# A decay-attention and MoE kernel: the last tokens' scores of two heads with one low-part product, decay rows copied by GpSimd, and a new order for some casts

## The chip, the cores and the metric

The kernel runs on one core of one Trainium2 chip. The metric is device time in microseconds: the median of the runs, 1192.13 us before the change (three runs, 1192.12 to 1192.14).

## The reference

Attention with a learned decay over 8 batches of 8 heads, 576 tokens and head size 64, in fp32; its output, with the heads side by side, is the input of a token mixing of low rank (`U`, `V`) and of a two-layer ReLU network with 512 and 2048 columns.

```python
scores = scale * np.matmul(q, k.transpose(0, 1, 3, 2))
cum = np.cumsum(np.log(np.clip(f, 0.0001, 1.0)), axis=-1)
decay = cum[:, :, :, None] - cum[:, :, None, :]
scores = np.where(causal, -1000000000.0, scores + decay)
attn = softmax(scores)          # with 1e-09 added to the sum
x = attn @ v                    # heads put side by side
u = x + (x.T @ U @ V).T
out = u + np.maximum(u @ w_ch1, 0.0) @ w_ch2
```

## The kernel before

**Pairs and steps.** The 64 heads are worked off as 32 pairs `p`, four to a batch. One pair is one step `t` of ten slots `s` (`step`, L852); its two heads are `j` 0 and 1. In step `t` the scores of pair `p` are computed while the probabilities of pair `p-1` are transposed and multiplied with V, and the results of pair `p-2` are turned back. Between these, TensorE gets parts of the network of an earlier batch (`filler`: `A` and `B` matmuls) and, in seven "mixing" steps (6, 10, 14, 18, 22, 26 and 30), the token mixing of the batch just finished. When the last pair is done, at about 670 us, the rest of the network runs alone.

**Scores.** The 576 tokens of a head are four blocks of 128 (`MAIN` = 512) and a tail of 64 (`TAIL`). `score(p, j, i)` writes the scores of block `i` of head `j` into a PSUM bank: `S_00` to `S_03` in slots 0 to 3, `S_10` at the end of slot 6, `S_11` to `S_13` in slots 7 to 9. `score_tail(p, x)` computes the tails of both heads in one bank, head 0 in rows 0 to 63 and head 1 in rows 64 to 127; `x` is the half of the 576 keys, so each half has 288 columns (`St_0` in slot 4, `St_1` in slot 5). One matmul of head 0 and one of head 1 add up in the bank: the query columns of the other head are zero. Each bank then goes to VectorE (`top`, L388 for blocks, L414 for tails: scale, mask and maximum), and to ScalarE for the exponential (L396, and L424 for tails, which makes `Ptl`).

**Two ways to multiply.** Pairs 0 to 5 (`p < NF`) multiply plain fp32 tiles (L364; the trace shows two matmul records for one such matmul). From pair 6 on, scores are the sum of two fp32r products: `G[0]` and `G[1]` (`G_91` and `G_92` in lists of instructions) hold four planes of 576 columns for head 0 and head 1. Plane 0 is the high part of q, plane 1 the low part of q in the head's own 64 rows and decay values in 4 of the other rows, plane 2 the high and low part of k, plane 3 the high part of k in the own rows and decay values in 4 others. The high product is plane 0 by plane 2 (L367), the low product plane 1 by plane 3 (L368), so the low product also adds the decay.

**Who fills `G`.** `parts(p, j, engines)` casts q and k (L330) and subtracts for the low parts (L345, L346, 64x576 each on GpSimd). ScalarE makes the 128x576 casts, save for pairs 11, 15, 19, 23, 27 and 31, the pairs behind a mixing step, where GpSimd does. Head 0's planes of pair `p+1` are made from slot 6 of step `p` on, when the tail has last read `G[0]`; head 1's planes of pair `p` from slot 0 of step `p` on, for `S_10`. Two DMAs per pair (`place_decay`, L351) write the decay rows from a DRAM table `cumd`.

**What sets the order.** TensorE's instructions stand in the order of the code, and SyncE's (which issues the DMAs, `SP`) in step 0 and from step 7 on; those of ScalarE, VectorE and GpSimd are ordered when the kernel is built, by the times that a scheduler simulates, save where the code pins them. GpSimd also makes `VS` (L199), parts of the turned results `xh` and `xl` (L630, L631) and, behind mixing steps, casts of the network's input (`uh`, `ul`, L688 and L689). The weights are decoded on VectorE in steps 0 to 7 (L72 to L89).

## Time and profile before

| what | value |
|---|---|
| median of three runs | 1192.13 us |
| the profiled execution's own time | 1192.27 us |
| its span in the trace | 1190.5 us |
| PE (TensorE matmul), busy | 1173.5 us, 8400 instructions |
| PEld (weight loads) | 91% |
| DVE (VectorE) | 76% |
| ACT (ScalarE) | 63% |
| POOL (GpSimd) | 47% |
| DMA | 116 GB/s over the span |
| granted TensorE clock | 1.0 in the whole span |

A busy share is an average over the span: how much of an engine's work sets the end has to be read from the chain of waits and from stretches. The sum of a prediction is made against the profiled execution's 1192.27 us, which is 0.14 us above the median; about 1.8 us of it lie outside the traced span.

### The profile page before, as it was taken

The page shows a single profiled execution, that of the slowest core. Times are in us where ns is not written, and L with a number is a line of the kernel's source. Part 1 is how long each engine was busy: PE and PEld are TensorE (multiplying, and loading weights), DVE is VectorE, ACT ScalarE, POOL GpSimd, SP SyncE. Part 2 cuts the span into 40 slices and gives each one's busy share as a digit, 9 for nine tenths or more (in the row PEclk, how much of TensorE's full clock was granted, in tenths as well). Part 3 has the DMA queues.
Part 4 walks back from the last instruction along what each step waited for, and adds up shares of the span by engine and source line. Part 5 has one row for each costly group of instructions (what it writes and reads, how often), then busy time and mean ns, then how long its engine had stood idle before and what let it go on. Part 6 is the DMA issues. An engine that isn't in the chain of part 4 may idle for free.

```text
span 1190.5 us, 23774 instructions
## 1 busy us (share of the span) xinstructions
PE 1173.5 (99%) x8400; PEld 1080.8 (91%) x8400; DVE 906.1 (76%) x2188; ACT 752.7 (63%) x2046; POOL 561.1 (47%) x588
## 2 busy tenths in 40 slices
PE   8999999999999999999999999999999999999998
PEld 5888899999899989989989997788999999999998
DVE  8988777677777677777676699966777767777675
ACT  8887786766868758767765577344454544545443
POOL 3315565546637447555553000024565555555554
PEclk9999999999999999999999999999999999999999
DMA  5754234434426425426332344542424344243421
GB/s 161 196 147 153 78 98 146 116 82 142 121 74 174 114 58 163 111 74 179 82 84 96 108 142 155 155 112 95 131 89 124 97 135 138 94 107 102 130 54 36
DMA packets 81431, 138.47 MB, mean 116 GB/s; under 512 B 8768, under 2 KB 46144, under 8 KB 79264
## 3 DMA queue, kind: packets, MB, share of 16 engines
q1 hardware_dynamic: 79680, 128.16, 36.1%
q0 software_dynamic: 1152, 8.39, 3.8%
q8 instruction: 66, 1.08, 0.4%
q14 instruction: 53, 0.43, 0.1%
q10 hardware_dynamic: 480, 0.40, 0.1%
HBM read 101.08 MB, written 35.78 MB: 115 GB/s over the span
## 4 chain that ended last, share of the span: by engine, by line
PE 85%; DVE 8%; ACT 4%; issue 2%; POOL 1%; DMA 0%; SPq 0%; ACTq 0%; DVEq 0%; POOLq 0%
PE N L1321 12%; PE B L775 12%; PE A L756 11%; PE A L1301 9%; PE B L1301 7%; PE V L579 6%; PE T L467 4%; PE S L367 3%; PE S L368 3%; PE O L1402 2%; PE B L1321 2%; PE V L544 2%; PE Tt L645 2%; PE S L364 1%; PE T_v L485 1%
## 5 line engine op out<-in xcount | busy, mean ns | idle before, releaser
L396 ACT ACTIVATE P<-S,nm 128x128 f32<-128x128 f32 (+3 forms) x256 | 138.0, 541 | 53.7 <-DVE nm L388 52.7
L199 POOL TENSOR_TENSOR hb<-xn,hb 128x256 fp32r<-128x256 f32 x136 | 111.6, 840 | 126.3 <-ACT hb L196 113.4
L388 DVE CUSTOM_DVE_ANT_0 S<-S,mask 128x128 f32<-128x128 f32 (+3 forms) x256 | 125.7, 497 | 52.5 <-PE S L368 48.6
L330 POOL CAST G<-qk 64x576 fp32r<-64x576 f32 (+1 forms) x76 | 50.6, 679 | 172.4 <-PE St L368 63.8
L756 PE MATMUL A<-uh,w1h 128*128 128x256 f32 (+1 forms) x384 | 119.8, 312 | 0.0
L756 PE MATMUL A<-ul,w1h 128*128 128x256 f32 (+1 forms) x384 | 113.6, 296 | 0.0
L756 PE MATMUL A<-uh,w1l 128*128 128x256 f32 (+1 forms) x384 | 113.5, 296 | 0.0
L196 ACT CAST hb<-xn 128x256 fp32r<-128x256 f32 x136 | 51.7, 404 | 84.7 <-DVE xn L1307 45.5
L775 PE MATMUL B<-w2h,hh 128*128 128x512 f32 x216 | 88.2, 408 | 0.0
L446 DVE TENSOR_TENSOR PTl<-T,PTh 128x512 fp32r<-128x512 f32 (+1 forms) x156 | 78.4, 527 | 9.6 <-ACT PTh L443 8.6
L467 PE MATMUL T<-ident,P 128*128 128x128 f32 x544 | 85.3, 272 | 0.0
L775 PE MATMUL B<-w2l,hh 128*128 128x512 f32 x216 | 85.0, 394 | 0.0
L775 PE MATMUL B<-w2h,hl 128*128 128x512 f32 x216 | 84.6, 392 | 0.0
L1321 PE MATMUL N<-sw,hb 128*128 128x256 f32 x546 | 79.9, 282 | 0.0
L1321 PE MATMUL N<-b2h,hb 128*128 128x256 f32 x420 | 79.8, 282 | 0.0
L345 POOL TENSOR_TENSOR G<-qk,G 64x576 fp32r<-64x576 f32 x52 | 74.7, 1437 | 10.8 <-issue 4.1
L346 POOL TENSOR_TENSOR G<-qk,G 64x576 fp32r<-64x576 f32 x52 | 75.0, 1442 | 6.6 <-ACT G L330 5.0
L367 PE MATMUL S<-G 128*128 128x128 f32 x208 | 70.9, 345 | 4.5 <-ACT P L396 3.3
L756 PEld LDWEIGHTS A<-uh,w1h 128*128 128x128 f32 x384 | 72.9, 190 | 0.9 <-DVE hl L761 0.2
L756 PEld LDWEIGHTS A<-uh,w1l 128*128 128x128 f32 x384 | 73.1, 190 | 0.5
L756 PEld LDWEIGHTS A<-ul,w1h 128*128 128x128 f32 x384 | 72.9, 190 | 0.0
L1321 PEld LDWEIGHTS N<-sw,hb 128*128 128x128 f32 x546 | 71.6, 190 | 0.0
(342 smaller groups left out, 3995.1 us busy)
## 6 DMA issues: line engine op xcount, KB each, us to landing
qk<-in_qk_dram SPq DMA_DIRECT2D x104, 288.0 KB
direct<-ud SPq DMA_DIRECT2D x48, 256.0 KB
sr<-in_w_dram SPq DMA_DIRECT2D x20, 512.0 KB
vr<-in_v_dram SPq DMA_DIRECT2D x32, 256.0 KB
accd<-ost SPq DMA_DIRECT2D x32, 256.0 KB
xn<-accd SPq DMA_DIRECT2D x8, 1024.0 KB
out_dram<-xn SPq DMA_DIRECT2D x30, 256.0 KB
ud<-uh SPq DMA_DIRECT2D x7, 1024.0 KB
```

Source lines behind the costliest of these rows:

```text
L199: leng.tensor_tensor(dl, src, dh.bitcast(F32), op=ALU.subtract)
L345: pin(el.tensor_tensor(g[oth, 2, cols], k[oth], gf[oth, 2, cols], op=ALU.subtract))
L346: pin(em.tensor_tensor(g[own, 1, cols], q[own], gf[own, 0, cols], op=ALU.subtract))
L367: nc.tensor.matmul(ps, G[j][:, 0, c0 : c0 + P], G[j][:, 2, cols], start=first, stop=False)
L388: newest["top"] = nc.vector.tensor_tensor_reduce(ps[:, :w], ps[:, :w], mask[:, 512 - w : 512], scale=-SCALE, scalar=3.0e38, op0=ALU.add, o ...
L396: nc.scalar.activation(pt, ps[:, :w], AF.Exp, bias=z["nm"][:, col : col + 1], scale=-1.0, accum_out=z["sm"][:, col : col + 1])
L446: defer(2, lambda: nc.vector.tensor_tensor(dstl, src, dsth.bitcast(F32), op=ALU.subtract))
L467: nc.tensor.transpose(tp[:, P * x : P * x + P], z["P"][j][i][:, P * c : P * c + P], ident)
L756: nc.tensor.matmul(ps[:, :nt], wt[:, fc, c], ut[:, c, sl], start=m == 0, stop=m == 3 * NDC - 1)
L775: nc.tensor.matmul(ps, ht[:, fc, P * x : P * x + P], wt[:, fc], start=fc == 0 and m == 0, stop=fc == NA - 1 and m == 2,)
L1301: nc.tensor.matmul(ps, a[x][:, c], b[y][:, c], start=start and m == 0, stop=m == 5, skip_group_check=not start)
L1321: nc.tensor.matmul(ps[:, y], a[p_][:, P * y : P * y + P], w[q_], start=start and y == 0 and m == 0, stop=stop and y == 1 and m == 2,)
```

## The change

Four things change around the tail's scores.

- **Pairs 2 to 5:** the two fp32 matmuls per half become one. GpSimd copies both heads' tail queries and keys into two joint tiles, `both_q` (64 rows per head, 64 columns each) and `both_k`, in slot 9 of the step before (`join_tail`, 64x64 and 64x576 per head).
- **Pairs 6 to 31:** the two low products per half become one. Its queries are in `G[0]` plane 1, where head 1's low tail queries now stand under head 0's (the subtract for them is a 64x64 piece of its own, the rest 64x512), its keys in `G[1]` plane 3, into whose free half a DMA copies head 0's high keys (`join_keys`). Since that half also held head 1's four decay rows, these are loaded into rows 96 to 99 of `G[0]` instead and copied by GpSimd (`next_decay`, 4x288 in slot 5 and 4x224 in slot 6) once the tail's matmuls have read the joint plane.
- **Decay of the tail:** it comes with the mask of VectorE's `top`. For each pair from 2 on two DMAs (slot 8 of the step before) broadcast one row per head from a DRAM table `based` into the 576 columns `lean` of the mask, and GpSimd adds the causal triangle to its last 64 columns in slot 2 (`lean_mask`, 128x64).
- **Order:** ScalarE's casts for the next pair's first head stand behind the newest ReLU as well as behind the newest tail exponential. Three loads of V per pair are pinned in steps 1 to 6, three tiles have another place, and the mask is cleared in two parts by VectorE and GpSimd.

```diff
+NO = 2
...
-    mask = att.tile([P, ZR + HW], F32, name="mask")
-    nc.vector.memset(mask, 0.0)
+    mask = att.tile([P, ZR + S], F32, name="mask")
+    nc.vector.memset(mask[:, 0:640], 0.0)
+    lean = mask[:, ZR:]
...
                 behind(cast, "tail")
+                if "relu" in newest:
+                    behind(cast, "relu")
...
-        pin(em.tensor_tensor(g[own, 1, cols], q[own], gf[own, 0, cols], op=ALU.subtract))
+        if j == 0:
+            pin(em.tensor_tensor(g[own, 1, cols], q[own], gf[own, 0, cols], op=ALU.subtract))
+            return
+        pin(em.tensor_tensor(G[0][own, 1, S : S + TAIL], q[own, 0:TAIL], gf[own, 0, TAIL:P], op=ALU.subtract))
+        pin(em.tensor_tensor(g[own, 1, P:], q[own, TAIL:S], gf[own, 0, P:], op=ALU.subtract))
+
+    def load_tail(p):
+        if not NO <= p < NP:
+            return
+        for j in range(2):
+            r = j * B * NHP + p
+            nc.sync.dma_start(lean[64 * j : 64 * j + 64], based[r : r + 1].broadcast_to([64, S]))
+
+    def join_tail(p):
+        if not NO <= p < NF:
+            return
+        for j in range(2):
+            q, k = st[p]["qk"][j]
+            at = AOFF[1] if j else MAIN
+            nc.gpsimd.tensor_copy(both_q[OWN[j], 64 * j : 64 * j + TAIL], q[0:64, at : at + TAIL])
+            nc.gpsimd.tensor_copy(both_k[OWN[j]], k[0:64])
+
+    def lean_mask(p):
+        if NO <= p < NP:
+            nc.gpsimd.tensor_tensor(lean[:, MAIN:S], lean[:, MAIN:S], tri, op=ALU.add)
+
+    ASIDE = slice(96, 100)
+
+    def next_decay(lo, hi):
+        nc.gpsimd.tensor_copy(G[1][0:4, 3, AOFF[1] + lo : AOFF[1] + hi], G[0].bitcast(F32)[ASIDE, 3, lo:hi])
+
+    def join_keys():
+        nc.sync.dma_start(G[1].bitcast(F32)[OTH[1], 3, COLS[1]], G[0].bitcast(F32)[OWN[0], 3, COLS[0]])
...
-            nc.sync.dma_start(G[j].bitcast(F32)[o : o + 4, 1:4:2, COLS[j]], cumd[r])
+            g = G[j].bitcast(F32)
+            if j == 0:
+                nc.sync.dma_start(g[o : o + 4, 1:4:2, 0:MAIN], cumd[r][:, :, 0:MAIN])
+                nc.sync.dma_start(g[ASIDE, 3, 0:MAIN], cumd[B * NHP + p][:, 1, 0:MAIN])
+            else:
+                nc.sync.dma_start(g[o : o + 4, 1, P:], cumd[r][:, 0, TAIL:S])
...
-        for j in range(2):
-            qk_mm(ps[:, :hw], p, ATAIL[j], cols, j == 0, j == 1, j)
+        if p < NO:
+            for j in range(2):
+                qk_mm(ps[:, :hw], p, ATAIL[j], cols, j == 0, j == 1, j)
+        elif p < NF:
+            nc.tensor.matmul(ps[:, :hw], both_q, both_k[:, cols], start=True, stop=True)
+        else:
+            at = [slice(AOFF[j] + cols.start, AOFF[j] + cols.stop) for j in range(2)]
+            for j in range(2):
+                nc.tensor.matmul(ps[:, :hw], G[j][:, 0, ATAIL[j] : ATAIL[j] + P], G[j][:, 2, at[j]], start=j == 0, stop=False)
+            nc.tensor.matmul(ps[:, :hw], G[0][:, 1, MAIN : MAIN + P], G[1][:, 3, at[1]], start=False, stop=True)
...
-                ps[:, :hw], ps[:, :hw], mask[:, x * ZR : x * ZR + hw], scale=-SCALE,
+                ps[:, :hw], ps[:, :hw], lean[:, hw * x : hw * x + hw], scale=-SCALE,
...
+                def relu():
+                    newest["relu"] = nc.scalar.activation(hh[:, fc, :nt], ps[:, :nt], AF.Relu)
...
+        nc.gpsimd.tensor_scalar(fl, fr, fr[:, MAIN - 1 : MAIN], -8.0, op0=ALU.subtract, op1=ALU.mult)
+        nc.sync.dma_start(based, fl)
...
                 place_decay(p, 1)
+                join_keys()
+            if s == 2 and ps_:
+                at(5, lambda: lean_mask(p))
...
+            if s == 5 and ps_ and p >= NF:
+                at(5, lambda: next_decay(0, HW))
+            if s == 6 and ps_ and p >= NF:
+                at(5, lambda: next_decay(HW, MAIN))
...
+            if s == 9 and ps_:
+                at(5, lambda: join_tail(p + 1))
...
+            if s == 8 and ps_:
+                load_tail(p + 1)
```

What this does to the order of the instructions is shown at three places.

TensorE in step 16, the tail of pair 16, before (`St_0` and `St_1` are the halves, `Ty` turns other results):

```order
L367 MATMUL St_0_4220<-G_91 128x288 [waits Activation_49]
L368 MATMUL St_0_4220<-G_91 128x288
L367 MATMUL St_0_4220<-G_92 128x288 [waits Pool_49]
L368 MATMUL St_0_4220<-G_92 128x288 [waits DMAHW0_49]
L507 MATMUL Ty_14_4225<-ident,Ptl_3986 64x128 [waits DVE_49]
L509 MATMUL Ty_14_4225<-ident,xT_4037 64x128
L367 MATMUL St_1_4237<-G_91 128x288 [waits Activation_49]
L368 MATMUL St_1_4237<-G_91 128x288
L367 MATMUL St_1_4237<-G_92 128x288
L368 MATMUL St_1_4237<-G_92 128x288
```

and now, with the first block of head 1, `S_10`, which stands further on in the same step:

```order
L464 MATMUL St_0_4309<-G_91 128x288 [waits Activation_49]
L464 MATMUL St_0_4309<-G_92 128x288 [waits Pool_49]
L465 MATMUL St_0_4309<-G_92,G_91 128x288 [waits DMAHW5_49]
L562 MATMUL Ty_14_4313<-ident,Ptl_4068 64x128 [waits DVE_49]
L564 MATMUL Ty_14_4313<-ident,xT_4121 64x128
L464 MATMUL St_1_4326<-G_91 128x288 [waits Activation_49]
L464 MATMUL St_1_4326<-G_92 128x288
L465 MATMUL St_1_4326<-G_92,G_91 128x288
...
L414 MATMUL S_10_4369<-G_92 128x128 [waits Activation_49]
L415 MATMUL S_10_4369<-G_92 128x128 [waits DMAHW4_49,Pool_49]
```

Two of eight matmuls are gone; the low product of `S_10`, which waited for nothing before, now has two waits, one for a DMA and one for GpSimd.

GpSimd in steps 16 and 17, from the split of V (`VS`) of one pair to the first cast for the next head, before:

```order
L199 TENSOR_TENSOR VS_4192<-vr_3939,VS_4192 128x10x64 [waits DMAHW2_49,DMAHW3_49,PE_49,DMAHW4_49,Activation_49,Pool_49]
L330 CAST G_91<-qk_0_4119 64x576 [waits DMAHW1_49,PE_49]
L630 TENSOR_TENSOR xh_4232<-xn_104,xh_4232 64x128 [waits Activation_49,Pool_49]
L631 TENSOR_TENSOR xl_4233<-xn_104,xh_4232 128x512 [waits Pool_49]
L436 TENSOR_TENSOR sm_4108<-sm_4108 128x1 [waits Activation_49]
L346 TENSOR_TENSOR G_91<-qk_0_4119,G_91 64x576 [waits Activation_49]
L345 TENSOR_TENSOR G_91<-qk_0_4119,G_91 64x576 [waits DMAHW2_49,Activation_49,Pool_49]
L330 CAST G_92<-qk_1_4266 64x576 [waits DMAHW0_49,PE_49]
```

and now:

```order
L204 TENSOR_TENSOR VS_4281<-vr_4022,VS_4281 128x10x64 [waits DMAHW4_49,PE_49,DMAHW5_49,Activation_49,Pool_49]
L336 CAST G_91<-qk_0_4207 64x576 [waits DMAHW6_49,DMAHW5_49,PE_49]
L385 CAST G_92<-G_91 4x288 [waits DMAHW1_49,PE_49,Pool_49]
L385 CAST G_92<-G_91 4x224 [waits PE_49]
L685 TENSOR_TENSOR xh_4321<-xn_107,xh_4321 64x128 [waits Activation_49]
L686 TENSOR_TENSOR xl_4322<-xn_107,xh_4321 128x512 [waits Pool_49]
L491 TENSOR_TENSOR sm_4194<-sm_4194 128x1 [waits Activation_49]
L355 TENSOR_TENSOR G_91<-qk_0_4207,G_91 64x576 [waits Activation_49]
L353 TENSOR_TENSOR G_91<-qk_0_4207,G_91 64x576 [waits DMAHW7_49,Activation_49,Pool_49]
L380 TENSOR_TENSOR mask<-mask,tri 128x64 [waits DMAHW0_49,DMAHW1_49,DVE_49,Pool_49]
L336 CAST G_92<-qk_1_4355 64x576 [waits DMAHW5_49,PE_49,Pool_49]
L357 TENSOR_TENSOR G_91<-qk_1_4355,G_92 64x64 [waits Activation_49]
```

The two copies of decay rows stand behind the first cast for the next pair, and the mask's triangle, which waits for the two broadcasts, ahead of the casts for head 1.

SyncE's queue from step 10 to step 11, before:

```order
L294 DMA qk_1_2499<-in_qk_dram 64x1152 [waits DMAHW5_49]
L294 DMA qk_1_2499<-in_qk_dram 64x1152 [waits DMAHW6_49]
L351 DMA G_91<-cumd 4x2x576 [waits DMAHW7_49,PE_49]
L351 DMA G_92<-cumd 4x2x576 [waits DMAHW0_49,PE_49]
L294 DMA qk_0_2623<-in_qk_dram 64x1152 [waits DMAHW1_49]
L294 DMA qk_0_2623<-in_qk_dram 64x1152 [waits DMAHW2_49]
```

and now:

```order
L299 DMA qk_1_2552<-in_qk_dram 64x1152 [waits DMAHW2_49]
L299 DMA qk_1_2552<-in_qk_dram 64x1152 [waits DMAHW3_49]
L395 DMA G_91<-cumd 4x2x512 [waits DMAHW4_49,PE_49]
L396 DMA G_91<-cumd 4x512 [waits DMAHW5_49,Pool_49]
L366 DMA mask<-based 64x576 [waits DMAHW6_49,DVE_49]
L366 DMA mask<-based 64x576 [waits DMAHW7_49]
L398 DMA G_92<-cumd 4x512 [waits DMAHW0_49,PE_49]
L388 DMA G_92<-G_91 64x576 [waits DMAHW1_49]
L299 DMA qk_0_2681<-in_qk_dram 64x1152 [waits DMAHW2_49]
L299 DMA qk_0_2681<-in_qk_dram 64x1152 [waits DMAHW3_49]
```

Four DMAs per pair are new (the aside rows, two broadcasts and the joint keys), and the queue waits for GpSimd and VectorE where it waited for TensorE alone.

## Rows read from the trace of the kernel before

**Rows 1.** The page: busy time by engine, and the chain's shares

```profile
PE 1173.5 (99%) x8400; PEld 1080.8 (91%) x8400; DVE 906.1 (76%) x2188; ACT 752.7 (63%) x2046; POOL 561.1 (47%) x588
...
PE 85%; DVE 8%; ACT 4%; issue 2%; POOL 1%; DMA 0%; SPq 0%; ACTq 0%; DVEq 0%; POOLq 0%
```

**Rows 2.** Busy time by engine in two stretches (start:end us, length, busy us)

```profile
37.60:50.50 12.90, 12.90 (x99) 11.36 (x98) 12.11 (x37) 10.05 (x32) 2.07 (x3) 1.00 0.84 214
125.00:642.00 517.00, 513.60 (x3612) 471.73 (x3610) 384.22 (x1109) 378.36 (x1084) 289.35 (x290) 1.00 0.41 113
```

**Rows 3.** PE's longest kind of wait, 125 to 642 us: total us, times, longest

```profile
PE S L367 <- ACT P L396: 2.1, 4, 0.9
```

**Rows 4.** Timeline of PE, pair 16's tail and second head (start us, us, ...)

```profile
312.15 0.29 PE L367 MATMUL St<-G 128*128 128x288 f32 x1
...
312.68 0.27 PE L507 MATMUL Ty<-ident,Ptl 128*64 128x128 f32 x1
...
317.08 0.22 PE L367 MATMUL S<-G 128*128 128x128 f32 x1
...
319.33 0.34 PE L367 MATMUL S<-G 128*128 128x384 f32 x1
```

**Rows 5.** Timeline of PE, pair 4's second tail half

```profile
69.05 1.14 PE L364 MATMUL St<-qk 128*128 128x288 f32 x4
70.02 0.27 PE L485 MATMUL T_v<-ident,Ptl 128*128 128x128 f32 x1
```

**Rows 6.** One line's instructions, L367: TensorE's waits that take an instruction each

```profile
L367 PEldq EVENT_SEMAPHORE  x26: 51/51/51, 90.4 to 621.1; - x26
```

**Rows 7.** Timeline of PE ahead of S_00 of pair 17

```profile
322.21 0.40 PE L775 MATMUL B<-w2l,hh 128*128 128x512 f32 x1
322.44 0.22 PE L367 MATMUL S<-G 128*128 128x128 f32 x1
```

**Rows 8.** Timeline of POOL in step 16

```profile
313.39 0.66 POOL L330 CAST G<-qk 64x576 fp32r<-64x576 f32 x1 [4.33 <-PE St L368]
315.08 0.46 POOL L630 TENSOR_TENSOR xh<-xn,xh 64x128 fp32r<-64x128 f32 x1 [1.03 <-ACT xh L629]
315.62 1.29 POOL L631 TENSOR_TENSOR xl<-xn,xh 128x512 fp32r<-128x512 f32 x1
...
318.61 1.43 POOL L345 TENSOR_TENSOR G<-qk,G 64x576 fp32r<-64x576 f32 x1
```

**Rows 9.** One line's instructions, L146 and L148: GpSimd clearing columns

```profile
L146 POOL MEMSET G<- x2: 574/715/856, 54.3 to 56.9; 64x576 f32 x2
...
L148 POOL MEMSET G<- x2: 567/710/853, 55.3 to 58.2; 4x576 f32 x2
```

**Rows 10.** Timeline of POOL in steps 10 and 11

```profile
187.68 1.88 POOL L330 CAST G<-qk 128x576 fp32r<-128x576 f32 x3 [9.93 <-PE St L367]
...
195.13 1.28 POOL L330 CAST G<-qk 128x576 fp32r<-128x576 f32 x2
...
202.20 1.44 POOL L345 TENSOR_TENSOR G<-qk,G 64x576 fp32r<-64x576 f32 x1
```

**Rows 11.** Timeline of PE, first tail matmul of pair 11

```profile
204.25 0.29 PE L367 MATMUL St<-G 128*128 128x288 f32 x1
```

**Rows 12.** Timeline of SP's queue at the end of step 10

```profile
189.84 6.10 SPq L351 DMA_DIRECT2D G<-cumd  x2
```

**Rows 13.** Chain of waits, one load's way from issue to landing

```profile
124.36 3.20 DMA qk<-in_qk_dram
```

**Rows 14.** Timeline of POOL at 7.6 us

```profile
7.63 1.56 POOL L166 TENSOR_TENSOR G<-dq,G 64x576 fp32r<-64x576 f32 x1 [1.29 <-DVE G L165]
```

**Rows 15.** Timeline of DVE at 8 and 10 us

```profile
7.86 1.38 DVE L177 TENSOR_SCALAR G<-G 32x64 fp32r<-32x64 f32 x1
...
10.06 0.18 DVE L177 TENSOR_SCALAR G<-G 32x64 fp32r<-32x64 f32 x1
```

**Rows 16.** Timeline of POOL at 37.7 us

```profile
37.73 1.82 POOL L631 TENSOR_TENSOR xl<-xn,xh 128x512 fp32r<-128x512 f32 x1
```

More of the change, by code (lines that the diff above doesn't have):

```diff
@@ L48, in tile_decay_attention_moe @@
     accd = nc.dram_tensor("accd", (NG, NM, P, DM), F32, kind="Internal").ap()
+    based = nc.dram_tensor("based", (B * H, S), F32, kind="Internal").ap()
     def words(ap):
@@ L127, in tile_decay_attention_moe @@
     COLS = tuple(slice(o, o + S) for o in AOFF)
-    mask = att.tile([P, ZR + HW], F32, name="mask")
-    nc.vector.memset(mask, 0.0)
+    mask = att.tile([P, ZR + S], F32, name="mask")
+    nc.vector.memset(mask[:, 0:640], 0.0)
+    lean = mask[:, ZR:]
+    tri = att.tile([P, TAIL], F32, name="tri")
+    both_q = att.tile([P, P], F32, name="both_q")
+    both_k = sb.tile([P, S], F32, tag="xT", name="both_k")
     blank = mask[:, 0:256].bitcast(mybir.dt.bfloat16)
@@ L146, in clear_operands @@
             tc.keep_in_program_order(nc.gpsimd.memset(g[OTH[j], 1, COLS[j]], 0.0))
-            tc.keep_in_program_order(nc.gpsimd.memset(g[OTH[j], 3, COLS[j]], 0.0))
-            tc.keep_in_program_order(nc.gpsimd.memset(g[ORW[j] : ORW[j] + 4, 1, COLS[j]], 1.0))
-            tc.keep_in_program_order(nc.gpsimd.memset(g[ORW[j] : ORW[j] + 4, 3, COLS[j]], 1.0))
+            if j == 0:
+                tc.keep_in_program_order(nc.gpsimd.memset(g[OTH[j], 3, COLS[j]], 0.0))
             z0 = (AOFF[j] + S) % 640
@@ L154, in decay_log @@
     def decay_log():
-        fr = sb.tile([B * H, S], F32, tag="xT", name="fr")
-        fl = sb.tile([B * H, S], F32, tag="cr", name="fl")
+        fr = sb.tile([P, 640], F32, tag="xh", name="fr")[0 : B * H, 0:S]
+        fl = sb.tile([P, S], F32, tag="cr", name="fl")[0 : B * H]
         return fr, fl, G[0][0 : B * H, :, 0:S], sb.tile([B * H, 2, S], F32, tag="VS", name="dq")
@@ L220, in load_w @@
             if fc % 2:
-                raw, a = spare[:, 1536:2560], sb.tile([P, 512], I32, tag="w2a", name=f"stg{u}")
+                raw, a = spare[:, 1536:2560], sb.tile([P, S], I32, tag="cr", name=f"stg{u}")[:, 0:512]
             else:
@@ L318, in load_v @@
         st[p]["vr"] = vr.rearrange("p c (j d) -> p c j d", j=2)
-        nc.sync.dma_start(vr[:, 0:NM], v[p, 0:MAIN].rearrange("(c p) d -> p c d", p=P))
+        pin = tc.keep_in_program_order if 0 < p < NF else lambda x: x
+        pin(nc.sync.dma_start(vr[:, 0:NM], v[p, 0:MAIN].rearrange("(c p) d -> p c d", p=P)))
         for r in range(2):
-            nc.sync.dma_start(vr[64 * r : 64 * r + 64, NM], v[p, MAIN:S])
+            pin(nc.sync.dma_start(vr[64 * r : 64 * r + 64, NM], v[p, MAIN:S]))
     def make_vs(p):
@@ L350, in place_decay @@
         if cm is None:
-            nc.sync.dma_start(G[j].bitcast(F32)[o : o + 4, 1:4:2, COLS[j]], cumd[r])
+            g = G[j].bitcast(F32)
+            if j == 0:
+                nc.sync.dma_start(g[o : o + 4, 1:4:2, 0:MAIN], cumd[r][:, :, 0:MAIN])
+                nc.sync.dma_start(g[ASIDE, 3, 0:MAIN], cumd[B * NHP + p][:, 1, 0:MAIN])
+            else:
+                nc.sync.dma_start(g[o : o + 4, 1, P:], cumd[r][:, 0, TAIL:S])
             return
@@ L573, in values @@
             z["xT"] = sb.tile([P, S], F32, tag="xT", name=f"xT{p}")
-        z["cr"] = sb.tile([D, S], F32, tag="cr", name=f"cr{p}_{j}")
+        z["cr"] = sb.tile([P, S], F32, tag="cr", name=f"cr{p}_{j}")[0:D]
         VS, xT, cr = z["VS"], z["xT"], z["cr"]
@@ L763, in low @@
                     )
-                defer(3, lambda: nc.scalar.activation(hh[:, fc, :nt], ps[:, :nt], AF.Relu), 1 + fine[0])
+                def relu():
+                    newest["relu"] = nc.scalar.activation(hh[:, fc, :nt], ps[:, :nt], AF.Relu)
+                defer(3, relu, 1 + fine[0])
                 defer(1, low, 2 + fine[0])
@@ L822, in tile_decay_attention_moe @@
         pad(1, 0)
+        nc.gpsimd.memset(mask[:, 640:], 0.0)
         nc.gpsimd.affine_select(mask[:, DG : DG + P], mask[:, DG : DG + P], [[-1, P]], ALU.is_ge, MASKED, base=0, channel_multiplier=1)
@@ L825, in tile_decay_attention_moe @@
             nc.gpsimd.affine_select(
-                mask[64 * j : 64 * j + 64, ZR + HW - TAIL :], mask[64 * j : 64 * j + 64, ZR + HW - TAIL :],
+                lean[64 * j : 64 * j + 64, MAIN:S], lean[64 * j : 64 * j + 64, MAIN:S],
                 [[-1, TAIL]], ALU.is_ge, MASKED, base=0, channel_multiplier=1,
@@ L848, in tile_decay_attention_moe @@
         load_w(3)
+        nc.gpsimd.tensor_copy(tri, lean[:, MAIN:S])
+        nc.gpsimd.memset(both_q, 0.0)
+        nc.gpsimd.tensor_scalar(fl, fr, fr[:, MAIN - 1 : MAIN], -8.0, op0=ALU.subtract, op1=ALU.mult)
+        nc.sync.dma_start(based, fl)
     mixing = []
```

## The prediction

> **What bounds the kernel now.** I read the page's totals first: TensorE is busy 99% of the span, and in the chain of waits it holds 85%, VectorE 8%, ScalarE 4%, GpSimd 1% [rows 1]. The reader should see that almost any TensorE work taken away shortens the kernel, if what feeds it keeps up. Then the stretches, since an average hides stages [rows 2]. From 125 to 642 us, the steady steps with fp32r scores, TensorE is busy 513.60 of 517.00 us and GpSimd 56%. In an early step with fp32 scores (37.60 to 50.50) TensorE is busy all the time, but VectorE, which still decodes weights, has 0.79 of 12.90 us free. Last the waits: in the steady stretch the largest kind is for ScalarE's exponentials, 2.1 us in all [rows 3]. So gains are read from TensorE's rows, and losses from the gap between the end of a feeding step and the matmul that needs it.
>
> **The fp32r tails.** Pair 16's first half starts at 312.15 and the next matmul at 312.68 [rows 4]: four matmuls in 0.53 us, 0.1325 each. A matmul's own duration (0.29) overlaps its neighbour, so the spacing is the price. The change takes two of eight per pair in 26 pairs: 52 x 0.1325 = **6.9 us**, all on TensorE.
>
> **The fp32 tails.** A half is 4 records from 69.05 to 70.02, 0.97 us for two matmuls [rows 5], so one is 0.485. Eight go (pairs 2 to 5, two halves): 8 x 0.485 = **3.9 us**. Gross gain 10.8 us.
>
> **Second waits on TensorE.** An instruction that needs two waits gets one of them as an instruction of its own, 51 ns in TensorE's queue [rows 6]. By the order of instructions the change adds 44 of these (the low products of `S_10` and `S_00` above all): at most 44 x 0.051 = 2.2 us. Below it may be nothing: the `B` matmul ahead of `S_00` starts at 322.21, `S_00` at 322.44 [rows 7], 0.23 apart as the spacing is for a 512-column matmul without a wait, so the queue can run ahead under a long matmul. The low product stands behind a short one (128 columns), which covers less; I take half, **1.1 us**, range 0 to 2.2.
>
> **GpSimd in the steady steps.** New per pair from 6 on: two copies of decay rows, a triangle add, and a subtract in two pieces. Rows cost nothing: clearing 4 rows of 576 columns takes 710 ns and 64 rows 715 [rows 9]; so a copy of 288 columns is half of the 0.66 us of a 64x576 cast [rows 8], 0.33, and one of 224 columns 0.26. A two-input operation takes 0.46 for 128 columns and 1.43 for 576 [rows 8], 2.2 ns a column on top of 0.18; hence 0.32 for the add and 0.18 for the extra piece. Sum 1.09 us a pair, 28 us in all, on an engine 56% busy. Who waits? The copies stand behind the cast that ends at 314.05 and end by my estimate at 314.7; `S_10` needs the first at 317.08 and `S_12` the second at 319.33 [rows 4, 8]. Over 2 us of room: cost nothing. The turned results behind them (`xh`, at 315.08) started after 1.03 us of idle time, so the copies fit ahead. If that cover were gone, each late copy would stop TensorE in front of `S_10`.
>
> **The six steps behind a mixing step** are the tight place. There GpSimd makes all casts for head 1: from 187.68 to 203.64 it has no real pause [rows 10], and the tail that needs its last subtract starts at 204.25 [rows 11], 0.61 us later (0.42 to 0.82 in the other five by the same reading). New in this run: the triangle add, 0.32, the extra piece, 0.18, and the wait of the add for the two broadcasts. SyncE issues the `cumd` DMA ahead of them at 189.84 [rows 12]; three more issues put the second broadcast at about 192.3, and a load takes 3.20 us to land [rows 13], so 195.5, 0.37 after the head's casts began (195.13). Together 0.87 against 0.61. I take 0.2 a step, **1.2 us**. Bounds: nothing (the scheduler's order leaves a little more room elsewhere) to 4 us (all of 0.87 lost in each step, less what the 0.13 per removed matmul moves).
>
> **New DMAs.** Four more per pair, of which the joint keys stand last, ahead of the loads of the next pair. Their copy is issued about 196 and by the same 3.20 us lands near 199.2, five microseconds ahead of the tail: nothing. Loads of q and k behind it move by some 2 us and are needed a step later: nothing.
>
> **The fp32 steps' GpSimd copies.** Four copies per pair, 2 x 0.66 and 2 x about 0.2, 1.7 us, on an engine busy 2.07 of 12.90 [rows 2]. It matters only through VectorE, which is nearly full there. A VectorE operation on 32x64 took 1.38 us while a two-input GpSimd operation ran from 7.63, and 0.18 alone [rows 14, 15]: these two engines do block each other. On the other hand GpSimd's `xl` took 1.82 at 37.73 among VectorE's decoding against 1.29 in step 16 [rows 8, 16], so there it was GpSimd that waited. I take **0.5 us** lost of the 3.9; bounds 0 and 2.
>
> The Trainium skill says in "SBUF — State Buffer", section "Who interferes with whom", that VectorE and GpSimd share one pair of ports as an exclusive lock, taken by VectorE's fast modes and by its operations with two SBUF inputs, and that the engine that comes second is blocked in full. The 1.38 us agree with it; by this rule all 1.7 us per pair could fall on VectorE, and the sum would be that of rival B.
>
> **The rest.** The order behind the ReLU moves ScalarE's casts a little later; the tail that needs them starts 3 us or more after they end in ordinary steps: nothing lost. It may free some of the 2.1 us of waits for exponentials; I take none and use 0.5 for the low end. Pinned loads, moved tiles, the split clear of the mask and the `based` table lie in the first steps beside other work: nothing.
>
> **Sum.** 6.9 + 3.9 - 1.1 - 1.2 - 0.5 = 8.0 us. The profiled execution's 1192.27 becomes 1184.3; it stands 0.14 above the median of the runs, so the median comes to **1184.1 us**. Low end: nothing lost and 0.5 freed, 1192.1 - 10.8 - 0.5 = 1180.8. High end: all bounds, 2.2 + 4 + 2 = 8.2 lost, 1189.5.
>
> **Rivals.** *B: VectorE is the bound of the fp32 steps.* If the copies block it, each of the four steps loses the 0.97 us gained and 1.7 - 0.79 = 0.9 on top: 3.9 + 3.6 of gain and time, against my 0.5; that gives 1191.1 in full, 1187.6 at half, the more likely size since one row shows GpSimd waiting. For: [rows 2, 15]; against: [rows 16]. *C: the change doesn't deliver.* TensorE waits where it used to multiply: ScalarE's exponentials free the score banks, and their waits already top the list [rows 3]; removed columns become waits, about 1192. Against: only 2.1 us in 517 are such waits, ScalarE is 63% busy. *D, the slower side: late broadcasts.* The triangle add is in front of all of GpSimd's casts behind a mixing step. If the broadcasts land not at 195.5 but after about 198 (SyncE's queue holds them behind an `aside` load that waits for GpSimd), the whole run from 195.13 shifts by 3 us and more, TensorE stops in front of the tail for that less the 0.61: 6 x 3 = 18 us lost, 1192.1 - 10 + 18 = 1200. It decides above some 2.5 us of lateness. Against: nothing ahead of them waits past 192.
>
> **Chances.** Forecast 0.78; B 0.10; C 0.07; D 0.05. The range from 1180.8 to 1189.5 takes in the forecast and half of B and leaves out C and D. A measurement here tells 0.2%, 2.4 us, from no change. Faster by more: the forecast and B at its likely size, 0.88; within: C, 0.07; slower: D, 0.05.
>
> **What would show it.** Right: `St` with three matmuls per half at 0.13 spacing, TensorE's busy time lower by about 10 us and still 99% of the span; `S_10` low starting 0.1 behind its high product; the tail in step 11 with a wait under 0.5 us. Wrong: waits of TensorE for GpSimd ahead of `St` or `S_10` over 1 us in ordinary steps (copies late), a triangle add that idles for a DMA for microseconds (D), an early step of 12.9 us or more with VectorE full and its two-input rows stretched (B), or waits for exponentials grown by as much as TensorE's work shrank (C). A time over 1189.5 means that one of these holds; under 1180.8 means that the new order on ScalarE freed more than the waits I see.

## The result and the profile after

The changed kernel takes **1201.59 us** in the median of six runs (1197.89 to 1204.88), against 1192.09 in six runs of the kernel before beside it (1192.02 to 1192.14): a ratio of 1.0078, interval 1.0059 to 1.0097. It is 9.5 us slower; I had forecast 1184.1, with at most 1189.5. The profiled execution is the slowest of the six, 1204.88 us; its span is 1203.1, 12.6 above that of before.

First the page: busy time by engine, the granted clock in 40 slices, the chain's shares and the DMA total.

```profile
PE 1175.5 (98%) x8332; PEld 1076.7 (89%) x8332; DVE 913.0 (76%) x2188; ACT 752.7 (63%) x2046; POOL 604.2 (50%) x711
...
PEclk9988999999999999999999999999999999999999
...
DMA packets 88497, 151.21 MB, mean 126 GB/s; under 512 B 10264, under 2 KB 47640, under 8 KB 86328
...
PE 64%; DVE 6%; ACT 1%; DMA 1%; issue 1%; SPq 1%; POOL 1%; DVEq 0%; ACTq 0%; POOLq 0%
```

TensorE has 68 records fewer (52 fp32r matmuls, and two records for each of eight fp32 ones) and is busy 2.0 us *longer* [rows 1]. Since matmuls were taken out, that isn't work; the clock line shows what it is: slices 3 and 4, from 60 to 120 us, are below full clock, where the kernel before had 1.0 throughout. 12.7 MB more are moved, 126 GB/s for 116.

Where in the program the time went shows in the start of a pair's first tail matmul, after minus before: -0.04 us at pair 2, +0.69 at 3, **+5.77** at 4, +5.22 at 5, **+9.12** at 6, +10.65 at 8, +13.95 at 16 and +13.03 at 31. So in the profiled execution nine of thirteen microseconds are lost in the steps with fp32 scores, where I had expected 3.4 of gain; from pair 6 to pair 31 another 3.9 are lost, where 25 steps with 0.265 less should gain 6.6.

**The early steps.** The timeline of PE has two waits there that before has not (there the same 20 matmuls start at 56.75, right behind the transposes):

```profile
59.16 3.73 PE L599 MATMUL V<-vr,PTh 128*128 128x64 f32 x20 [1.86 <-DMA vr<-in_v_dram]
...
92.96 3.44 PE L599 MATMUL V<-vr,PTh 128*128 128x64 f32 x20 [1.22 <-DMA vr<-in_v_dram]
```

TensorE waits for V's load. And the busy time by engine in three stretches (start:end, length, PE, PEld, DVE, ACT, POOL, then granted clock, DMA share, GB/s):

```profile
49.00:59.00 10.00, 7.89 (x51) 6.13 (x50) 9.45 (x32) 9.37 (x30) 3.30 (x5) 1.00 1.00 234
60.00:66.50 6.50, 6.50 (x29) 5.79 (x28) 2.91 (x7) 0.37 (x1) 3.22 (x8) 0.50 0.37 98
94.00:101.00 7.00, 7.00 (x35) 6.29 (x35) 2.21 (x6) 2.05 (x8) 4.01 (x5) 0.51 0.65 181
```

The second price is larger than the wait: about a microsecond after TensorE takes up work again the granted clock is 0.50, its 1.2 GHz level, for 6.8 us, from 60.0 to 66.8, and so again from 94.1 to 101.0. A stretch of 6.8 us at half clock holds 3.4 us of work: 3.4 lost, behind a wait of 1.86.

Why V is late shows in SP's queue after:

```profile
47.78 0.68 SPq L187 DMA_DIRECT2D cumd<-fl  x1
48.50 0.61 SPq L188 DMA_DIRECT2D cumd<-fl  x1
49.16 0.82 SPq L189 DMA_DIRECT2D cumd<-G  x1
50.03 1.41 SPq L190 DMA_DIRECT2D cumd<-G  x1
51.48 1.40 SPq L236 DMA_DIRECT2D xn<-in_w_dram  x1
52.99 1.38 SPq L303 DMA_DIRECT2D qk<-in_qk_dram  x1
54.47 0.53 SPq L325 DMA_DIRECT2D vr<-in_v_dram  x1
...
58.85 1.17 SPq L366 DMA_DIRECT2D mask<-based  x2
```

and in that of before:

```profile
43.22 0.68 SPq L182 DMA_DIRECT2D cumd<-fl  x1
...
52.45 0.53 SPq L319 DMA_DIRECT2D vr<-in_v_dram  x1
```

The four stores of the decay table start 4.6 us later. While they run, from 49 to 59 us, the DMA engines are full (share 1.00). V's load is issued only 2.0 us later than before, but into that burst, and lands at 59.1, 4.7 us after its issue; before, TensorE took V up 4.3 us after the issue and had not waited for it.

**The fp32r steps.** The longest kinds of wait of PE from 125 to 642 us (total us, times, longest):

```profile
PE S L414 <- ACT P L443: 4.0, 6, 1.4
PE S L415 <- DMA G<-cumd: 2.3, 4, 1.0
PE Tt L700 <- DVE PTl L501: 1.8, 3, 1.2
PE T_v L522 <- DVE xT L654: 1.4, 3, 0.6
```

Before, ScalarE's exponentials are the head of this list with 2.1 [rows 3] and the other three are not on it. But between these fixed times the changed kernel, being late, is at an earlier place of the program: from pair 6's first tail to pair 31's, the same part of both, the exponentials are 3.3 before and 4.0 now, and the other three still only now. What I forecast for the matmuls themselves did come; the timeline of PE at pair 16, to be held against [rows 4]:

```profile
326.10 0.42 PE L464 MATMUL St<-G 128*128 128x288 f32 x2
326.36 0.29 PE L465 MATMUL St<-G,G 128*128 128x288 f32 x1
326.49 0.27 PE L562 MATMUL Ty<-ident,Ptl 128*64 128x128 f32 x1
...
330.75 0.22 PE L414 MATMUL S<-G 128*128 128x128 f32 x1
330.81 0.28 PE L415 MATMUL S<-G 128*128 128x128 f32 x1
```

Three matmuls in 0.39 us, 0.13 each; the low product of `S_10` 0.06 behind its high one, without a wait. Ordinary steps, away from the mixing steps, are 0.15 to 0.27 us shorter than before. What is lost is lost at few places: 1.5 between pairs 6 and 8, 1.5 between 11 and 12, 2.5 between 15 and 16. Between pairs 6 and 31 TensorE's idle time grows from 5.6 to 12.0 us and its busy time falls only from 524.16 to 521.69.

### The profile page after: what moved, and what is told of

Read it like the earlier page. It is cut to its first block, busy times and chain, and to the rows that moved or that the text cites. A ratio compares the mean times of both kernels' runs of the same rounds, so it can differ in the third digit from the quotient of the medians.

```text
span 1203.1 us, 24063 instructions
## 1 busy us (share of the span) xinstructions
PE 1175.5 (98%) x8332; PEld 1076.7 (89%) x8332; DVE 913.0 (76%) x2188; ACT 752.7 (63%) x2046; POOL 604.2 (50%) x711
## 3 DMA queue, kind: packets, MB, share of 16 engines
q8 instruction: 66, 1.08, 0.4%
## 4 chain that ended last, share of the span: by engine, by line
PE 64%; DVE 6%; ACT 1%; DMA 1%; issue 1%; SPq 1%; POOL 1%; DVEq 0%; ACTq 0%; POOLq 0%
PE N L1395 12%; PE A L1375 9%; PE B L833 8%; PE A L811 8%; PE B L1375 7%; PE V L634 4%; PE T L522 2%; PE O L1476 2%; PE B L1395 2%; PE S L414 2%; PE S L415 2%; DMA G<-cumd 1%; PE O L1239 1%; PE Tt L700 1%; PE Tx L665 1%
## 5 line engine op out<-in xcount | busy, mean ns | idle before, releaser
L353 POOL TENSOR_TENSOR G<-qk,G 64x576 fp32r<-64x576 f32 x52 | 74.5, 1433 | 14.1 <-PE T L522 6.2
L522 PEld LDWEIGHTS T<-ident,P 128*128 128x128 f32 x544 | 66.9, 142 | 5.2 <-issue 2.0
```

What stands on the lines that cost most here:

```text
L353: pin(el.tensor_tensor(g[oth, 2, cols], k[oth], gf[oth, 2, cols], op=ALU.subtract))
L522: nc.tensor.transpose(tp[:, P * x : P * x + P], z["P"][j][i][:, P * c : P * c + P], ident)
```

## The experiments

The table has the median, the ratio to the kernel before with its interval, and from each trace the start of the first tail of pairs 4, 6 and 31 against before (us). The changed kernel's own row stands first. "NO = 6" leaves the fp32 tails of pairs 2 to 5 as they were.

| kernel | median | ratio | pair 4 | 6 | 31 |
|---|---|---|---|---|---|
| the change | 1201.59 | 1.0078 [1.0059, 1.0097] | +5.77 | +9.12 | +13.03 |
| e2_no6 | 1194.18 | 1.0016 [1.0007, 1.0025] | -0.22 | -0.40 | +0.90 |
| e4_lean_act | 1212.07 | 1.0163 [1.0148, 1.0178] | +4.40 | +4.83 | +20.08 |
| e6a_no_bcast | 1195.86 | 1.0029 [1.0014, 1.0043] | +5.26 | +3.94 | +6.68 |
| e6b_no_copies | 1200.78 | 1.0063 [1.0046, 1.0080] | +5.19 | +3.96 | +8.65 |
| e7_store_late | 1195.18 | 1.0027 [1.0015, 1.0039] | +0.30 | +2.78 | +5.22 |
| e8_no6_no_relu | 1194.94 | 1.0022 [1.0012, 1.0032] | +2.11 | +1.95 | +3.47 |
| e9_no6_no_lean | 1196.18 | 1.0030 [1.0018, 1.0043] | +2.41 | +2.25 | +5.96 |
| e10_before_two_stores | 1202.82 | 1.0088 [1.0073, 1.0103] | +11.22 | +11.05 | +11.02 |
| e11_before_drop_low | 1188.90 | 0.9974 [0.9965, 0.9984] | -0.02 | -0.04 | -3.60 |
| e12_before_drop_fp32 | 1191.03 | 0.9992 [0.9983, 1.0002] | -0.53 | -1.24 | -0.95 |
| e13_no6_no_next | 1197.00 | 1.0051 [1.0032, 1.0070] | +0.29 | +0.11 | +4.19 |
| e14_no6_noeps | 1189.80 | 0.9983 [0.9974, 0.9992] | -0.54 | -0.60 | -3.18 |
| e15_no6_noeps_sub | 1189.88 | 0.9978 [0.9969, 0.9987] | -0.08 | -0.25 | -1.99 |
| e16_before_noeps | 1191.11 | 0.9991 [0.9982, 1.0000] | -0.01 | -0.02 | -1.18 |
| e17_noeps | 1199.35 | 1.0053 [1.0038, 1.0069] | +6.08 | +4.72 | +7.98 |
| e18_ul_first | 1187.84 | 0.9968 [0.9956, 0.9979] | -0.06 | -0.23 | -4.22 |
| e19_after_ul_first | 1198.05 | 1.0049 [1.0032, 1.0066] | +5.14 | +4.20 | +6.20 |

### Which part, and is it SyncE's queue

`e2_no6` takes the change's tails out of pairs 2 to 5, `e4_lean_act` issues the broadcasts from ScalarE's queue instead of SyncE's.

```diff
-NO = 2
+NO = 6
```
```diff
-            nc.sync.dma_start(lean[64 * j : 64 * j + 64], based[r : r + 1].broadcast_to([64, S]))
+            nc.scalar.dma_start(lean[64 * j : 64 * j + 64], based[r : r + 1].broadcast_to([64, S]))
```

> The joint fp32 tails of pairs 2 to 5 are undone (NO = 6), with their copies and broadcasts; pairs 6 to 31 stay as changed. Theory 1 (the loss arises in the first six steps): the first tail of pair 6 starts within 1 us of the kernel before (100.7 us in its trace, 109.8 in the changed one), no stretch at half clock, total 1189 to 1194 us. Rival (the loss is spread over the fp32r steps): total stays at 1198 or more.

> The broadcasts of the tail's decay rows are issued on ScalarE's queue instead of SyncE's; bytes and everything else stay. Theory 1a (V comes late because SyncE's queue is held up): no wait of TensorE for the V loads, clock 1.0, 1188 to 1193 us. Theory 1b (V comes late because the DMA engines are full): waits for V of over 1 us and a stretch at half clock remain, 1197 us or more.

Without the early part no V is waited for, though it lands only 0.13 us before its matmul at 56.46, and the median drops by 7.4 us: the main loss is there. What is left is still 2 us slower than before. Another queue helps nothing: the waits for V stay (1.50 and 1.41), and in the fp32r steps 10.0 us of waits for decay rows come on top, the two longest (2.2 us, at 487 and 573 us) with 3.4 us at half clock each. It is not the issuing that is short, or not alone.

### Broadcasts, copies, or the burst of stores

`e6a_no_bcast` leaves out the broadcasts for pairs 3 to 5, `e6b_no_copies` the joint tiles' copies for them; `e7_store_late` keeps all work and puts the stores of the decay table six slots later.

```diff
-        if not NO <= p < NP:
+        if not NO <= p < NP or NO < p < NF:
```
```diff
-        if not NO <= p < NF:
+        if p != NO:
```
```diff
-            if (t, s) == (3, 2):
+            if (t, s) == (3, 8):
```

> Pairs 3, 4 and 5 load no decay rows for the tail (they use pair 2's; six DMAs of 64x576 less), all copies and products stay. Theory 1 (broadcasts make V late): no wait for V, full clock, first tail of pair 6 at 99 to 101 us, total 1188 to 1193. Rival 2 (GpSimd's copies hold up VectorE): little changes, 1198 or more.

> Pairs 3, 4 and 5 make no joint copies of q and k (they use pair 2's; twelve GpSimd operations less), all broadcasts and products stay. Theory 1: the waits for V and the half clock remain, 1197 us or more. Rival 2 (copies against VectorE): they go, 1188 to 1193.

> The changed kernel, in which the four stores of the decay table to DRAM are asked for six slots later, so that three of them are issued behind the load of V for pair 2 (ahead of it in the changed kernel). Theory 3 (added DMAs push this burst of stores onto the load of V, TensorE waits and its clock falls): the wait at 59 us goes, first tail of pair 4 at 66 to 69 us (73.74 before this edit, 67.97 in the kernel before), total 1193 to 1197. Rival (ScalarE's order is what V waits for): the wait of about 1.9 us stays, 1199 or more.

Neither without the broadcasts (a pause of 1.55 us) nor without the copies (2.12) does the first pause go; so it is not VectorE blocked by GpSimd's copies, my rival B. (The profile puts these two pauses down to ScalarE, whose semaphore rose last, but by the semaphore events of the DMA V's load landed 0.13 us before the matmul in both, as in the change.) Both edits do let the stores start earlier: at 45.92 without the broadcasts and 46.17 without the copies, against 47.78 in the change, 44.08 in `e2_no6` and 43.22 before. With the stores moved the pause is gone. SP's queue and PE in `e7_store_late`:

```profile
51.27 0.53 SPq L325 DMA_DIRECT2D vr<-in_v_dram  x1
...
53.67 0.66 SPq L188 DMA_DIRECT2D cumd<-fl  x1
```
```profile
57.05 2.35 PE L599 MATMUL V<-vr,PTh 128*128 128x64 f32 x20
59.23 1.11 PE L603 MATMUL V<-vr,PTh 128*128 128x128 f32 x8
```

V's load stands ahead of three of the four stores, the 20 matmuls take 2.18 us (3.52 in the changed kernel, by the next row's start there at 62.68) and pair 4 is only 0.30 late: 5.5 us are back. The load is also issued 3.2 us earlier here (51.27 against 54.47), so this run doesn't tell its place in the queue from the full DMA engines. The second wait, near 90 us, doesn't come in every trace: 1.22 in the profiled run of the change, 1.84 here, none in `e6a_no_bcast`, nor in `e17_noeps`, where VectorE, ScalarE and GpSimd have the order of the change until past 120 us. There the load is issued at 85.94 (85.87 in the change) and the row of PE reads

```profile
91.90 2.34 PE L600 MATMUL V<-vr,PTh 128*128 128x64 f32 x20
```

So the lost second wait of `e6a_no_bcast` shows nothing of the broadcasts. It may explain a part of the spread among the six runs of the change, of which only one has a trace: with it pair 6 is 9.1 late, without it 3.9 to 4.7 (`e6a_no_bcast`, `e6b_no_copies`, `e17_noeps`, `e19_after_ul_first`), and the mean granted clock of those six goes from 0.994 (the profiled one) to 0.997.

### The same loss made in the kernel before

If late V and the clock are the cause, a kernel without any part of the change must show them once its burst of stores is made longer. `e10_before_two_stores` stores the table a second time, into a table that nobody reads.

```diff
+        for table in (cumd, cumd2):
+            nc.sync.dma_start(table[:, 0:2, 0], two)
...
-        nc.sync.dma_start(cumd[:, 0:2, 0], two)
```

> The kernel before, with the four stores of the decay table done twice (the second time to a table that nobody reads), at the same place; nothing of the change is in it. Theory 3: the doubled burst delays the load of V for pair 2 by 3 us or more, TensorE waits over 1.5 us for it and then runs at half clock for some microseconds: 1197 to 1203 us. Rival (a late load is not enough, or the clock falls for another reason): full clock throughout and at most the length of the wait, under 1196.

It does. PE waits for V, and in the stretch behind, by the columns of the stretches above, the clock is at half:

```profile
63.84 4.50 PE L546 MATMUL V<-vr,PTh 128*128 128x64 f32 x20 [6.91 <-DMA vr<-in_v_dram]
```
```profile
62.50:72.00 9.50, 8.16 (x34) 7.48 (x35) 1.33 (x4) 0.00 (x0) 0.20 (x1) 0.50 0.17 44
```

All later pairs are 11.0 to 11.2 late: 6.9 of waiting and 4.2 of half clock, and nothing of it comes back.

### What the removed matmuls are worth by themselves

Two kernels before with only the removal: `e11_before_drop_low` leaves out head 0's low product in the tails from pair 6 on, `e12_before_drop_fp32` head 0's matmul in the tails of pairs 2 to 5.

```diff
+            nc.tensor.matmul(ps[:, :hw], G[1][:, 1, ATAIL[1] : ATAIL[1] + P], G[1][:, 3, at[1]], start=False, stop=True)
```
```diff
+        if 2 <= p < NF:
+            qk_mm(ps[:, :hw], p, ATAIL[1], cols, True, True, 1)
```

> The kernel before, with head 0's low product of the tail left out for pairs 6 to 31 (52 matmuls fewer, the tail's low part and decay of head 0 missing); nothing is added: no copies, broadcasts, joint keys. Theory D (the time TensorE gains is real, and what the change adds to feed the joint product eats it): 1185 to 1186.5 us. Theory E (TensorE runs into the next engine behind it, VectorE or ScalarE, so the removal alone does not pay): 1189 or more, with new short waits for VectorE or ScalarE around the mixing steps.

> The kernel before, with head 0's fp32 matmul of the tail left out for pairs 2 to 5 (8 matmuls fewer, head 0's tail scores missing); nothing is added. If the fp32 steps have room on the other engines: 1188 to 1189 us. If VectorE, ScalarE and the loads set the pace there: 1191 to 1193, the saved time turned into waits; above 1194 the load of V comes late here too.

Of 6.9 us come 3.6 (in the trace, pair 6 to 31), of 3.9 come 1.2, although nothing was added. In the fp32 steps TensorE then waits, 0.5 us for V and 0.3 for exponentials from 52 to 101 us, where before no wait is listed: what feeds it was nearly as late as itself. In `e11_before_drop_low` 1.2 us are lost at one place at pair 8, in whose step the last weights are decoded; rows of DVE, and of PE:

```profile
129.76 1.85 DVE L78 TENSOR_TENSOR w2l<-stg,w2h 128x512 fp32r<-128x512 f32 x1
```
```profile
132.46 0.27 PE L651 MATMUL Tt<-xh,Us 128*64 128x128 f32 x1 [1.18 <-DVE PTl L452]
```

The subtract took 0.68 us in the kernel before. Here GpSimd runs a two-input operation from 129.66 to 131.06, and the subtract ends 0.5 after it: VectorE was held for nearly the whole of it. The changed kernel has the same row with 1.86, and a wait of 1.20 behind it. The order that the scheduler makes has shifted so that the two meet.

### The steps with scores from fp32r: which addition costs

All on the kernel with `NO = 6`: `e8_no6_no_relu` without the order behind the ReLU, `e9_no6_no_lean` without broadcasts and triangle, `e13_no6_no_next` without the copies of decay rows.

```diff
-                if "relu" in newest:
-                    behind(cast, "relu")
```
```diff
-        if NO <= p < NP:
+        if p < 0:
```
```diff
-        nc.gpsimd.tensor_copy(G[1][0:4, 3, AOFF[1] + lo : AOFF[1] + hi], G[0].bitcast(F32)[ASIDE, 3, lo:hi])
+        pass
```

> NO = 6 (fp32 tails as before), and ScalarE's casts no longer ordered behind the newest ReLU. Theory A (that order costs nothing or helps): 1193 to 1196 us as with NO = 6 alone (1194.2). Theory B (it makes the small new waits in the steps around mixing): 1188 to 1191.

> NO = 6, and no decay rows at all for the tails: neither the broadcasts nor GpSimd's triangle add for any pair (the tails' decay is left out); joint product, joint keys and copied decay rows stay. Theory C (the lean rows, by GpSimd's late add and SyncE's queue, eat the gain of the fp32r steps): 1186 to 1189 us. Rival (the copies of decay rows and the joint keys eat it): 1192 or more.

> NO = 6, without GpSimd's two copies of decay rows per pair (head 1's low product then has wrong rows in plane 3); broadcasts, triangle add, joint keys stay. Theory D in its GpSimd form (the copies delay GpSimd's other work): 1190 us or less. Otherwise as with NO = 6 alone, 1193 to 1196.

None is faster than `e2_no6` (1194.18), two are 2 to 3 us slower with less work. In two of them a part is lost ahead of pair 6: TensorE pauses 2.03 us for ScalarE at 27 us in `e8_no6_no_relu` and 1.08 at 57 us in `e9_no6_no_lean`, there by the same semaphore events until V's load has landed; 3.4 us at half clock follow, so that pair 6 starts 2.4 and 2.7 later than in `e2_no6`. From pair 6 to 31 the traces have 531.06 us in `e2_no6`, 531.28, 533.47 and 533.84 in the three, and 529.76 before. So none of these three additions is by itself the price (the joint keys and the subtract in two pieces were not taken out); each edit makes another order of VectorE's, ScalarE's and GpSimd's instructions. The trace of `e9_no6_no_lean` shows what such an order can cost: each of the six steps behind a mixing step is 0.9 to 1.1 us longer than before. Its rows of DVE, and of POOL:

```profile
200.78 1.31 DVE L492 TENSOR_SCALAR sm<-sm 128x9 f32<-128x9 f32 x1 [0.92 <-ACT P L443]
202.12 0.22 DVE L493 RECIPROCAL rv<-sm 128x9 f32<-128x9 f32 x1
```
```profile
200.77 1.29 POOL L744 TENSOR_TENSOR ul<-full,uh 128x512 fp32r<-128x512 f32 x1
```

Adding 1e-9 to nine columns takes 1.31 us, since it starts 0.01 us after a GpSimd subtract and ends with it; VectorE's next work is late, and TensorE waits for `xT`. In the changed kernel the groups of VectorE's instructions, 125 to 642 us, have that add at (busy us, mean ns | idle before)

```profile
L492 DVE TENSOR_SCALAR sm<-sm 128x9 f32<-128x9 f32 x24 | 12.6, 525 | 15.8 <-ACT P L443 13.9 <-POOL G L336 1.8
```

and before at

```profile
L437 DVE TENSOR_SCALAR sm<-sm 128x9 f32<-128x9 f32 x24 | 6.9, 286 | 10.0 <-ACT P L396 9.9
```

### Without the add

`e17_noeps` is the changed kernel without that add from pair 6 on, `e16_before_noeps` the control on the kernel before, `e14_no6_noeps` has `NO = 6` and the late stores as well, and `e15_no6_noeps_sub` also gives the last weights' subtract to GpSimd.

```diff
-        nc.vector.tensor_scalar(sm[:, 0:9], sm[:, 0:9], 1e-9, None, op0=ALU.add)
+        if p < NF:
+            nc.vector.tensor_scalar(sm[:, 0:9], sm[:, 0:9], 1e-9, None, op0=ALU.add)
```

> The changed kernel without VectorE's addition of 1e-9 to the sums for pairs 6 to 31 (sums are at least 1, so fp32 results stay the same). Theory F (VectorE's 128x9 addition is held up to 1.3 us while GpSimd reads SBUF, and its delay makes the small waits behind the mixing steps): the time from the first tail of pair 6 to that of pair 31 falls from 533.7 us to 529 to 531, no 1.2 us operation of VectorE on the sums is left. Rival (these waits come from ScalarE and the loads): 533 or more. The first six steps stay as they are, total 1196 to 1201.

> The kernel before without that addition, as a control: nothing of it was held up there (no such operation over 0.6 us after 125 us), so 1191.5 to 1192.5 us. If 1190 or less, leaving it out is a gain of its own and no evidence on the change.

> NO = 6 (fp32 tails as before), no addition of 1e-9 from pair 6 on, decay stores asked for six slots later. Theory F with theory 3: 1189 to 1191.5 us, less than both kernels. Rival: 1193 or more, as NO = 6 alone.

> As the run before, and the last decoded weight chunk's two additions go to GpSimd, so that VectorE's subtract of 0.7 us, which took 1.86 us beside a GpSimd subtract in step 7, is gone. Theory F: the wait of 1.2 us of TensorE for VectorE at about 133 us goes, 1188 to 1190.5 us. Rival: the wait only moves, same as the run before.

The add alone is worth 0.65 us from pair 6 to 31 on the changed kernel (3.91 lost become 3.26) and 1.2 on the kernel before. There 0.9 of it come between pairs 6 and 7, and in that place the kernel before has an add that is held too, which I had overlooked; rows of DVE and of POOL before:

```profile
114.80 1.40 DVE L437 TENSOR_SCALAR sm<-sm 128x9 f32<-128x9 f32 x1
```
```profile
114.40 1.76 POOL L345 TENSOR_TENSOR G<-qk,G 64x576 fp32r<-64x576 f32 x1
```

So a held add can cost TensorE about a microsecond, but I had called it the cause of the waits in the changed kernel, and for most of them it isn't. In `e17_noeps` the waits go elsewhere, 4.7 us for decay rows in place of 2.3. In `e14_no6_noeps`, with another order, 2.6 us are gained from pair 6 on. The subtract on GpSimd only moves the wait (1.0 at 130.69).

### Late decay rows

In the changed kernel the wait for decay rows stands in the steps behind a mixing step. The rows of POOL and of SP's queue in step 11:

```profile
205.84 0.32 POOL L380 TENSOR_TENSOR mask<-mask,tri 128x64 f32<-128x64 f32 x1 [0.80 <-DMA mask<-based]
...
214.69 0.65 POOL L336 CAST G<-qk 64x576 fp32r<-64x576 f32 x1
215.32 1.28 POOL L744 TENSOR_TENSOR ul<-full,uh 128x512 fp32r<-128x512 f32 x1
```
```profile
216.62 0.36 SPq L782 DMA_DIRECT2D ud<-ul  x1
...
222.17 0.68 SPq L395 DMA_DIRECT2D G<-cumd  x1
```

and PE behind them:

```profile
228.33 0.30 PE L415 MATMUL S<-G 128*128 128x128 f32 x1 [1.01 <-DMA G<-cumd]
```

SyncE's store of `ul` waits for GpSimd, which now makes `ul` behind the casts for the next pair; the queue behind the store is late with it: the store is issued 1.95 us after the step's first tail matmul, before 0.67 (204.92, against 204.25 in [rows 11]). The decay rows stand last in that queue. `e19_after_ul_first` is the changed kernel with one order more: the cast for the next pair's first head stands behind `ul`. `e18_ul_first` has it on top of `e14_no6_noeps`.

```diff
-        pin(copy(ek2, g[own, 3, cols], k[own]))
+        high = pin(copy(ek2, g[own, 3, cols], k[own]))
+        if j == 0 and "ul" in newest:
+            behind(high, "ul")
```

> The version with NO = 6, no addition of 1e-9 and later decay stores (1189.8 us), in which GpSimd's first cast for the next pair stands behind its last subtract for the network's input (ul) behind a mixing step, as in the kernel before. Theory G (a late ul holds up SyncE's store of it, and with it the loads of V, of q and k and of the decay rows behind it in the queue, for which the low product of S_00 then waits): the store of ul and the decay rows are issued 0.6 us earlier, the waits for decay rows (0.2 to 0.8 us, three times) go, 1187.5 to 1189 us. Rival: the waits move to the tails' first matmul (GpSimd), 1189.5 or more.

> The changed kernel with that edit alone. Theory G: the stretch from the first tail of pair 6 to that of pair 31 falls from 533.7 us to 531 to 532.5, the waits for decay rows (2.3 us in all) to under 0.7; the first six steps stay, total 1198 to 1201. Rival: 533 or more.

The waits for decay rows are gone from `e19_after_ul_first` (2.3 to none), and the stretch from pair 6 to 31 is 1.9 us shorter. That is with 3.4 us at half clock from 137.4, behind a pause of 1.20 that ends at 137.14; the changed kernel has that pause at 142 with full clock. From pair 8 to 31, behind it, the stretch is 3.4 shorter. `e18_ul_first` is the fastest of all, 1187.84, faster than both kernels, but without the joint fp32 tails and the add; its longest kinds of wait from 125 to 642 us:

```profile
PE S L416 <- ACT P L445: 1.9, 3, 0.9
PE Tt L703 <- DVE PTl L504: 1.8, 3, 1.2
PE S L417 <- DMA G<-cumd: 0.9, 2, 0.5
```

## Why the prediction was wrong

- **"New DMAs. Four more per pair ... nothing": the step that failed.** It was priced by its issue and landing in the fp32r steps, and the early steps by GpSimd's copies alone, with all else there "beside other work: nothing". In the early steps the burst of stores slid by 4.6 us into V's load, whose tile is a single buffer and had no slack. Measured: some 5.5 us at the first place (1.86 of wait, 3.4 by the clock), and at the second, in the traces where it occurs, 3.9 more in the change, 3.0 in `e7_store_late` and 0.9 in `e4_lean_act`, whose clock stayed at 1.00 there. Shown by `e7_store_late`, which takes the first away, and by `e10_before_two_stores`, which makes it in the kernel before. Of the 4.6 us, 1.9 go without the broadcasts of pairs 3 to 5 and 1.6 without their copies, by the start of the stores; leaving out either did not suffice. The pinned loads of V stand in `e2_no6` too, where no V is waited for, so they alone don't do it; what they add in the change is not shown, since no run leaves them out.
- **The clock** stood in no term and no rival: it was 1.0 throughout in the table of the profile before and in [rows 2], and I took it as given. In the profiled execution it costs 6.8 us, more than the two waits for V, 3.1.
- **The fp32 tails, "3.9":** the spacing of 0.485 was right, the gain was not: 1.2 with the removal alone (`e12_before_drop_fp32`).
- **The fp32r tails, "6.9":** 0.13 a matmul is confirmed, and ordinary steps gain 0.15 to 0.27. But the removal alone brings 3.6 from pair 6 to 31; part of the rest became waits, 1.2 at one place, and those for ScalarE's exponentials grew from 3.3 to 4.5, which is rival C in part.
- **"Second waits, 1.1":** too much; ordinary steps are 0.265 shorter at best, as without any.
- **The six steps behind mixing, "1.2":** the broadcast did arrive late (the triangle add waited 0.80 us in step 11), but the larger loss was another one, my rival D's mechanism at a different load: SyncE's queue held by a store of `ul`, 2.3 us.
- **"Fp32 copies, 0.5" and rival B:** without the copies the first pause stays, and the median is only 0.8 us lower. By the first tail of pair 3, ahead of the pause, the copies may cost some 0.7: it is 0.69 late in the change and 0.07 early without them. VectorE and GpSimd do hold each other up, but the rows found are in the decoding and the sums: 1.31 us for an add of nine columns. The Trainium skill, "SBUF — State Buffer", section "Who interferes with whom", says that the engine that comes second is blocked in full; here both VectorE rows end with GpSimd's operation or a time of their own after it, so the trace agrees.
- **The order behind the ReLU, "none":** right within what the runs tell, 1194.94 against 1194.18.

In the stretch from pair 6 to 31, 10.5 us are missing against my sum (3.9 lost, 6.6 expected). 6.4 of them are idle time of TensorE, and the other 4.1 are busy rows that didn't shrink as they should. Of the whole, 1.9 answer to the order of `ul`, or 3.4 where the half clock of that run is left out. How the rest splits among the orders of VectorE, ScalarE and GpSimd is not settled, since every edit makes a new order.
